# Chunked attention ahead of an expert layer: state summed from PSUM, the mask and a one-hot on ScalarE, a PSUM bank for VectorE's operands

## The chip, the cores and the metric

The kernel runs on one core of a Trainium2 chip. The metric is the device time of one launch in microseconds (us); lower is better. Five engines work side by side, each through its own list of instructions in order: TensorE (PE), VectorE (DVE), ScalarE (ACT), GpSimd (POOL), and SyncE (SP), whose list here is the queue of nearly all DMAs.

## The reference, cut to what matters

Three layers, one after the other. With B=4, H=8, S=768, D=40 the first is a recurrent attention; its output is 3072 tokens of 320 numbers.

```python
for t in range(S):
    m_new = np.maximum(f_gate[:, :, t] + m, i_gate[:, :, t])
    f_stab = np.exp(f_gate[:, :, t] + m - m_new)
    i_stab = np.exp(i_gate[:, :, t] - m_new)
    C = f_stab * C + i_stab * outer(vt, kt)
    n = f_stab * n + i_stab * kt
    y[:, :, t] = sigmoid(o_gate) * (C @ qt) / np.maximum(np.abs(n . qt), 1.0)
# expert layer: top 1 of 8 experts, d_ff 1024
logits = xn @ en.T / tau            # rows of x and expert_emb normalized
e = argmax(logits); gate_w = softmax(logits)[e]
out = gate_w * (relu(x @ w1[e]) @ w2[e])
# rational layer, d_ff 2048
h = x @ w_in
g = (a0 + a1 h + a2 h^2 + a3 h^3) / (1 + |b0||h| + |b1| h^2 + 1e-6)
return g @ w_out
```

## The kernel before, in words

**Attention.** The 3072 tokens are 24 tiles of 128 (tile t is chunk c = t % 6 of batch b = t // 6). Within a tile the recurrence is a product with a decay matrix: `s_scan` (L560) builds, for all eight heads, the 128 x 1024 matrix d of running products of the forget gates from fb, a broadcast of one tile's gates to all partitions (`load_f`, L351), and eight identities side by side. `s_score` (L337) makes the scores k·q in three matmuls, into three PSUM banks (phs[0], yb[0], yb[1]); `s_p` (L602) multiplies them into d, in three pieces; `s_out` multiplies by v (L621), adds the product of the carried state with the decayed q (qd, L629), and makes pc, this tile's addition to the state (L637). `s_state` carries the state on: pc has the products of all pairs of heads of a group of three, so the ones off the diagonal are masked out (L655, tm = pc * bmask), and cn = cn * fcol + tm in three pieces, one for each group of heads (L658). Where c is 0, one masked product makes cn (L652); where c is 5, there is no state to carry.

Each finished tile is then divided by its denominator (`s_abs` L674, `s_den1`, `s_den2`, `s_w` on POOL, `s_x` L693), transposed (`s_tr` L709), and routed: `s_logit` (L720), the winning expert oh (`s_arg`, L731 to L741), the position within the expert by two tiny matmuls, with a triangle and with ones (`s_rank` L753), and the running count (`s_count` L758). `s_pos` (L765 to L788) turns rank into two one-hot matrices, ohp (L781, 128 wide: the column in its group of 128) and ohj (L788), whose product (`s_map` L798) scatters token numbers into a map from position to token. `s_store` writes the tile to memory.

**What sets the order.** The loop `for step in range(-4, 24)` goes through a list written by hand, `plan`, of entries (lag, function): in each step every function runs for tile step - lag. The scan has lag -1, scores and s_p lag 0, s_out and s_state lag 1, the division lag 2, transposes 3, logits 4, the winner and s_rank 5, s_pos 6, s_map 7. What an engine gets in a step stands in its list in that order, and an instruction that waits holds up all behind it on its engine. Entries dv, pv, av take single instructions from side lists (the expert norms, the expert order, the first weights).

Ahead of the loop stands a prologue written out by hand (gates, their products, the first two tiles' scans and scores), behind it a drain, which finishes the last tiles and mixes in the first matmuls of the first expert (`pre_split` L257 transposes its gathered rows xj; `pre1`). The expert layer follows (w_load, `w_hi` L185, gemm1 L1471), with products of values split in high and low parts (`mm3`, L230), then the rational layer. `coef_load` and `dbl_load` start the transfers of the rational layer's coefficients and first weights; before, they are written behind the block that counts the tokens of each expert (L1527 to L1557).

## Time and profile before

| | us |
|---|---|
| runs of the kernel before | 820.78, 818.58, 820.72 (median 820.72) |
| the profiled execution, whole | 818.65 |
| its span, as the profile counts | 816.8 |
| busy in the span: PE, DVE, ACT, POOL | 762.5, 711.1, 489.7, 579.5 |

The span runs from the first to the last instruction that the profiler records; the time of the execution is 1.85 us longer. An engine's busy share is an average over three layers with different limits, so the rows further down are read stage by stage: prologue up to about 28 us, the loop to about 172, drain and first expert to about 222, the experts to about 350, the rational layer to the end. A row of a timeline gives the start and the length of a run of equal instructions (x3: three of them), the line, the operation, and output <- inputs with partitions x elements; in brackets stands the idle time of the engine before it and whom it waited for. The length counts to the end of the last one; since instructions overlap a little, the distance from one start to the next is what the engine spends.

### The profile page before, as it was taken

Reading aid. Unit: us, or ns where it says so; the run is one execution under the profiler, and the core shown is the slowest. Engines: PE = TensorE matmul, PEld = TensorE weight load, DVE = VectorE, ACT = ScalarE, POOL = GpSimd, SP = SyncE. Lnnn points to the kernel's source line nnn. Section 1 sums busy time; section 2 is a strip of 40 time slices with the busy share of each in tenths; the row PEclk is TensorE's granted clock in tenths of the full one; section 3 lists DMA queues with packets and bytes.
Section 4 is the critical chain, followed back from the end, with each engine's and each line's share of the span. In section 5 each row is a group of like instructions: output and inputs, shape, how many; then the busy total and the mean of one; then the engine's idle time right before and its main releaser. Section 6 shows DMA issues by size and latency. Waiting matters only on the chain.

```text
span 816.8 us, 14477 instructions
## 1 busy us (share of the span) xinstructions
PE 762.5 (93%) x4724; PEld 711.6 (87%) x4724; DVE 711.1 (87%) x1421; ACT 489.7 (60%) x839; POOL 579.5 (71%) x595
## 2 busy tenths in 40 slices
PE   8998888878789999999999899999999999999994
PEld 5787777768788788999999799999999999999983
DVE  7999999998669999998788898989888888889882
ACT  5344334433345655555657787787787877777872
POOL 6554443465447668679963688989899888989883
PEclk7899999988889999999999899999999999999998
DMA  8998787931747667688765030101000010000000
GB/s 199 263 233 248 222 240 214 263 114 49 209 121 212 198 180 225 201 272 270 251 206 187 1 118 21 42 1 49 1 26 25 17 33 9 17 9 17 1 25 24
DMA packets 86960, 102.37 MB, mean 125 GB/s; under 512 B 7915, under 2 KB 79219, under 8 KB 86880
## 3 DMA queue, kind: packets, MB, share of 16 engines
q1 hardware_dynamic: 82976, 88.63, 37.6%
q0 software_dynamic: 3904, 12.77, 4.8%
q8 instruction: 38, 0.62, 0.3%
q14 instruction: 42, 0.34, 0.1%
HBM read 84.01 MB, written 17.93 MB: 125 GB/s over the span
## 4 chain that ended last, share of the span: by engine, by line
PE 57%; DVE 21%; DMA 7%; issue 6%; POOL 4%; ACT 2%; SPq 2%; POOLq 0%; DVEq 0%; ACTq 0%
PE h L230 21%; PE yb L1308 6%; PE yb L1310 6%; PE ph L230 6%; PE yb L1309 6%; PE yb L1486 2%; PE yb L1487 2%; PE yb L1488 2%; DVE cn L658 2%; DVE ohp L781 1%; DMA raw<-in_w_in 1%; DMA r<-in_w 1%; POOL l L194 1%; DMA fb<-fz_d 1%; DVE xt L693 1%
## 5 line engine op out<-in xcount | busy, mean ns | idle before, releaser
L1248 POOL TENSOR_TENSOR U<-U,A 128x768 f32<-128x768 f32 (+1 forms) x65 | 119.0, 1830 | 30.8 <-ACT U L1240 26.1
L1310 PE MATMUL yb<-wo,gl 128*128 128x320 f32 x384 | 119.4, 311 | 1.8 <-POOL gl L1294 1.7
L1308 PE MATMUL yb<-wo,gh 128*128 128x320 f32 x384 | 119.2, 310 | 1.2 <-ACT gh L1291 1.2
L1294 POOL TENSOR_TENSOR gl<-P,gh 128x768 fp32r<-128x768 f32 x63 | 117.7, 1868 | 3.6 <-ACT gh L1291 3.0
L1309 PE MATMUL yb<-wo,gh 128*128 128x320 f32 x384 | 119.0, 310 | 0.0
L1224 ACT ACTIVATE P<-h,coef 128x768 f32<-128x768 f32 (+1 forms) x65 | 64.0, 984 | 73.4 <-PE h L230 73.4
L230 PE MATMUL h<-xh,winh 128*128 128x384 f32 x256 | 90.9, 355 | 3.9 <-DVE P L1257 3.8
L194 POOL TENSOR_TENSOR l<-r,h 128x384 fp32r<-128x384 f32 x64 | 63.7, 1017 | 38.5 <-ACT h L185 38.4
L1252 DVE TENSOR_TENSOR P<-P,h 128x768 f32<-128x768 f32 (+1 forms) x65 | 61.2, 942 | 29.6 <-ACT A L1232 24.9
L230 PE MATMUL h<-xh,winl 128*128 128x384 f32 x256 | 86.7, 339 | 0.0
L230 PE MATMUL h<-xl,winh 128*128 128x384 f32 x256 | 86.7, 339 | 0.0
L1310 PEld LDWEIGHTS yb<-wo,gl 128*128 128x128 f32 x384 | 72.5, 189 | 2.6 <-POOL gl L1294 2.6
L1308 PEld LDWEIGHTS yb<-wo,gh 128*128 128x128 f32 x384 | 72.6, 189 | 1.5 <-ACT gh L1291 1.5
L1309 PEld LDWEIGHTS yb<-wo,gh 128*128 128x128 f32 x384 | 72.5, 189 | 0.0
L1242 POOL TENSOR_SCALAR U<-A,coef 128x768 f32<-128x768 f32 x56 | 54.9, 981 | 21.9 <-ACT A L1232 21.2
L1486 PE MATMUL yb<-h,hh 128*128 128x320 f32 (+1 forms) x216 | 67.5, 313 | 3.0 <-DVE ysb L1500 3.0
L1487 PE MATMUL yb<-l,hh 128*128 128x320 f32 (+1 forms) x216 | 67.2, 311 | 0.0
L1257 DVE SCALAR_TENSOR_TENSOR P<-P,coef,h 128x768 f32<-128x768 f32 (+1 forms) x65 | 65.2, 1003 | 2.3
L1488 PE MATMUL yb<-h,hl 128*128 128x320 f32 (+1 forms) x216 | 67.0, 310 | 0.0
L1283 DVE SCALAR_TENSOR_TENSOR P<-P,coef,s 128x768 f32<-128x768 f32 (+1 forms) x62 | 62.0, 1000 | 1.7
L1275 DVE SCALAR_TENSOR_TENSOR U<-U,s 128x768 f32<-128x768 f32 (+1 forms) x62 | 58.0, 935 | 4.7 <-ACT s L1271 4.6
L230 PE MATMUL ph<-xh,h 128*128 128x256 f32 (+4 forms) x152 | 55.8, 367 | 6.4 <-DVE hl L1472 5.8
(590 smaller groups left out, 2322.4 us busy)
## 6 DMA issues: line engine op xcount, KB each, us to landing
fb<-fz_d SPq DMA_DIRECT2D x22, 512.0 KB
r<-in_w SPq DMA_DIRECT2D x32, 320.0 KB
r<-in_w SPq DMA_DIRECT2D x32, 256.0 KB
raw<-in_w_out SPq DMA_DIRECT2D x16, 320.0 KB
r<-in_w SPq DMA_DIRECT2D x64, 64.0 KB
raw<-in_w_in SPq DMA_DIRECT2D x32, 128.0 KB
x_rows<-xt SPq DMA_DIRECT2D x24, 164.5 KB
xt<-y_sorted SPq DMA_DIRECT2D x8, 481.5 KB
```

What stands on the lines that cost most here:

```text
L194: eng.tensor_tensor(out=l1[:, :, sl], in0=r1[:, :, sl], in1=h1[:, :, sl].bitcast(F32), op=ALU.subtract)
L230: mms = [nc.tensor.matmul(ps, lhsT=a, rhs=b, start=(i == 0), stop=(i == 7)) for i, (a, b) in enumerate(seq)]
L1224: r = nc.scalar.activation(out=part("P", m, i), in_=part("ph", m, i), func=AF.Identity, scale=coef[:, 3:4], bias=coef[:, 2:3])
L1248: eng.tensor_tensor(out=U, in0=U, in1=part("A", m, i), op=ALU.mult)
L1257: r = nc.vector.scalar_tensor_tensor(out=P, in0=P, scalar=coef[:, 1:2], in1=part("ph", m, i), op0=ALU.add, op1=ALU.mult)
L1294: eng.tensor_tensor(out=part("gl", m, i), in0=part("P", m, i), in1=part("gh", m, i).bitcast(F32), op=ALU.subtract)
L1308: nc.tensor.matmul(y, lhsT=gh[:, i, t], rhs=wh, start=first, stop=False)
L1309: nc.tensor.matmul(y, lhsT=gh[:, i, t], rhs=wl, start=False, stop=False)
L1310: nc.tensor.matmul(y, lhsT=gl[:, i, t], rhs=wh, start=False, stop=last)
L1486: nc.tensor.matmul(y, lhsT=hh[:, js], rhs=h2[:, half, :], start=(fb == 0), stop=False)
L1487: nc.tensor.matmul(y, lhsT=hh[:, js], rhs=l2[:, half, :], start=False, stop=False)
L1488: nc.tensor.matmul(y, lhsT=hl[:, js], rhs=h2[:, half, :], start=False, stop=(fb == NFB - 1))
```

## The change

It has six parts.

1. The state is summed straight from PSUM: cn = cn * fcol + pc, with no mask ahead of it and no tm. The mask moves behind it, to ACT: `s_mask` makes cm, the masked copy, in three products, and qd·c reads cm. `s_state` stands ahead of the scan.
2. The scores go into two banks instead of three, in four matmuls (384, 128, 256, 256 wide), and s_p multiplies two pieces of 512. The bank yb[1] that comes free is VectorE's: it holds three identities (vid), jt and the small tiles key, sj and dn. The scan is cut in three, over 3, 3 and 2 heads, with vid as its second operand.
3. ohp moves from VectorE to ACT, as two operations: dist = |iota + sj|, then Relu(tokf - tokf * dist).
4. `s_rank` moves from the end of lag 5 to lag 6, behind the scores; `s_map` behind the logits; in the drain the last `s_out` comes ahead of the last map, and `s_pre` behind both.
5. fz_d in memory is laid out by tiles, so that the load of fb is one row of 4 KB for each partition; the store of it is four DMAs for one, twice.
6. The prologue has the scans and scores of tiles 0 and 1 and s_out(0) ahead of the second half of the gates, with ten small idle products; `coef_load` and two `dbl_load` are written ahead of the counts.

```diff
@@ state, mask
             if c == 0:
-                nc.vector.tensor_tensor(out=cn, in0=pc, in1=mk, op=ALU.mult)
+                nc.vector.tensor_copy(cn, pc)
             else:
-                tm = lp.tile([120, H * V], F32, name="tm", bufs=1)
-                nc.vector.tensor_tensor(out=tm, in0=pc, in1=mk, op=ALU.mult)
                 for g, (h0, n) in enumerate(GR):
                     sl = slice(h0 * V, (h0 + n) * V)
                     nc.vector.scalar_tensor_tensor(
-                        out=cn[:, sl], in0=st["c", t][:, sl], scalar=fcol[:, b, g, c:c + 1], in1=tm[:, sl],
+                        out=cn[:, sl], in0=st["cn", t - 1][:, sl], scalar=fcol[:, b, g, c:c + 1], in1=pc[:, sl],
                         op0=ALU.mult, op1=ALU.add,
                     )
...
+        def s_mask(t):
...
+            for j in range(3):
+                hs = slice(j, H, 3)
+                nc.scalar.activation(
+                    out=ch[:, hs, :], in_=cv[:, hs, :], func=AF.Copy, scale=bmask[:, 0, j, 0:1]
+                )
+            st["c", t + 1] = cm
@@ the bank, scores, scan
+    vid, vjt, vkey, vsj, vdn = (
+        sr["yb"][1][:, a:a + n] for a, n in ((0, HALF), (384, JS), (392, NE), (400, 1), (408, H))
+    )
...
-        for g, (h0, n) in enumerate(GR):
...
+        pss = [v.rearrange("p (h t) -> p h t", t=CH) for v in (phs[0], sr["yb"][0])]
+        for g, h0, n in ((0, 0, 3), (1, 3, 1), (1, 4, 2), (2, 6, 2)):
...
-            nc.vector.tensor_tensor_scan(
-                out=d_.rearrange("p h t -> p (h t)"), data0=fb.rearrange("p h t -> p (h t)"),
-                data1=ident8.rearrange("p h t -> p (h t)"), initial=0.0, op0=ALU.mult, op1=ALU.add,
-            )
...
+            for h0, n in GR:
+                sl = slice(h0 * CH, (h0 + n) * CH)
+
+                nc.vector.tensor_tensor_scan(
+                    out=df[:, sl], data0=ff[:, sl], data1=(ident3 if t < 2 else vid)[:, 0:n * CH], initial=0.0,
+                    op0=ALU.mult, op1=ALU.add,
+                )
@@ fb and its store
-        fv = fz_d[b * H:(b + 1) * H, c * CH:(c + 1) * CH]
-        nc.sync.dma_start(out=fb, in_=fv.unsqueeze(0).broadcast_to([128, H, CH]))
+        nc.sync.dma_start(
+            out=fb.rearrange("p h t -> p (h t)"), in_=fz_d[t:t + 1, :].broadcast_to([128, H * CH])
+        )
...
-            nc.sync.dma_start(out=fz_d[:, a:z], in_=fzf[:, a:z])
+            for b in range(B):
+                nc.sync.dma_start(
+                    out=fz_d[b * NCH + ca:b * NCH + cz, :].rearrange("c (h t) -> h c t", t=CH),
+                    in_=fz[b * H:(b + 1) * H, ca:cz, :],
+                )
@@ one-hot
-                nc.vector.tensor_scalar(
-                    out=st["ohp", t], in0=niota, scalar1=st["sj", t][:, 1:2], scalar2=tokf[:, t:t + 1],
-                    op0=ALU.is_equal, op1=ALU.mult,
+
+                dist = ap.tile([128, 128], F32, name="dist", bufs=1)
+                nc.scalar.activation(out=dist, in_=iota, func=AF.Abs, bias=st["sj", t][:, 1:2])
+                nc.scalar.activation(
+                    out=st["ohp", t], in_=dist, func=AF.Relu, scale=ntokf[:, t:t + 1], bias=tokf[:, t:t + 1]
                 )
@@ plan
-            at(1, s_out), at(3, s_tr), at(4, s_logit), at(5, s_rank), at(5, s_keep),
-            at(-1, s_scan), dv, at(1, s_state), at(3, s_trc), at(2, s_x2),
+            at(1, s_out), at(3, s_tr), at(4, s_logit), at(7, s_map), at(7, s_first), at(5, s_keep),
+            at(1, s_state), at(-1, s_scan), dv, at(3, s_trc), at(2, s_x2), at(1, s_mask),
@@ drain
+        s_pos(z - 6, 3)
+        s_out(z)
+        s_map(z - 6)
+        s_abs(z)
+        s_pre(z)
         pre1(0)
-        s_map(z - 6)
-        s_out(z)
-        s_abs(z)
@@ rational layer
+        coef_load()
+        for i in range(2):
+            dbl_load(i)
 
         tc.mark_branch_hint_location("over", "LikelyTaken", mybir.ALL_ENGINES)
```

How it moves the instructions shows in three lists. First VectorE, one step in the middle of the loop, before (d is the decay matrix, ph the bank of pc, sj and ohp belong to the positions):

```order
L693 TENSOR_TENSOR xt<-pa,sg 128x320
L560 SCALAR_TENSOR_TENSOR d__1491<-fb,ident_97 128x1024
L655 TENSOR_TENSOR tm<-ph_119,bmask 120x328
L658 SCALAR_TENSOR_TENSOR cn<-cn,fcol,tm 120x123 x2
L658 SCALAR_TENSOR_TENSOR cn<-cn,fcol,tm 120x82
...
L776 SCALAR_TENSOR_TENSOR sj<-sj,rank 128x1
L602 TENSOR_TENSOR d__1491<-yb_113,d__1491 128x384
L781 TENSOR_SCALAR ohp<-niota,sj,tokf 128x128
```

The same place with the change:

```order
L730 TENSOR_TENSOR xt<-pa,sg 128x320
...
L678 SCALAR_TENSOR_TENSOR cn<-cn,fcol,ph_120 120x123 x2
L678 SCALAR_TENSOR_TENSOR cn<-cn,fcol,ph_120 120x82
L585 SCALAR_TENSOR_TENSOR d__1675<-fb,yb_115 128x384 x2
L585 SCALAR_TENSOR_TENSOR d__1675<-fb,yb_115 128x256
...
L814 SCALAR_TENSOR_TENSOR sj<-yb_115,rank 128x1
L627 TENSOR_TENSOR d__1675<-yb_114,d__1675 128x512
```

The state stands ahead of the scan, tm and ohp are gone, and scan, cn and sj have an operand in PSUM (yb_115 and ph_120 are banks).

Then TensorE, from the products for the state through the next scores, before:

```order
L637 MATMUL ph_119<-v_1418,n__1257 120x123 x2
L637 MATMUL ph_119<-v_1418,n__1257 120x82
L709 MATMUL px<-ident,xt 128x128 x3
L720 MATMUL plr<-enT,xT 128x8 x3
L753 LDWEIGHTS tri
L753 MATMUL plr<-oh,tri 128x8
L753 LDWEIGHTS ones
L753 MATMUL plr<-oacc,ones 128x8
L337 MATMUL ph_118<-bd,k__1178 128x384
L337 MATMUL yb_113<-bd,k__1178 128x384
L337 MATMUL yb_114<-bd,k__1178 128x256
```

And with the change:

```order
L746 MATMUL px<-ident,xt 128x128 x3
L757 MATMUL plr<-enT,xT 128x8 x3
L838 MATMUL plr<-ohj,ohp 128x32 x2
L343 MATMUL ph_119<-bd,k__1247 128x384
L343 MATMUL ph_119<-bd,k__1247 128x128
L343 MATMUL yb_114<-bd,k__1247 128x256 x2
L790 LDWEIGHTS tri
L790 MATMUL plr<-oh,tri 128x8
L790 LDWEIGHTS ones
L790 MATMUL plr<-oacc,ones 128x8
```

The rank's two matmuls have gone behind the scores, and the map's two ahead of them.

Last ACT, one step, with the change (before, it has none of cm, dist and ohp):

```order
L821 ACTIVATE dist<-iota,sj 128x128
L822 ACTIVATE ohp<-dist,tokf,ntokf 128x128
L707 ACTIVATE dn<-pa 128x8
L700 ACTIVATE sg<-n__1509 128x320
L783 ACTIVATE xt<-plr 128x8
L751 ACTIVATE xT<-px 128x384
L738 ACTIVATE sg,xt<-xt 128x320
L692 ACTIVATE cm<-cn,bmask 120x3x41 x2
L692 ACTIVATE cm<-cn,bmask 120x2x41
```

The mask's three products stand last in the step, behind the copy of the transposes and the squares of xt.

## Rows read from the trace of the kernel before

**Rows 1.** Windows: busy us (and instructions) of each engine, granted clock, DMA share, GB/s.
```profile
28.00:172.00 144.00, 127.74 (x888) 108.81 (x887) 141.89 (x407) 52.65 (x146) 65.83 (x113) 0.98 0.79 224
172.00:222.00 50.00, 41.39 (x269) 38.05 (x270) 41.89 (x154) 17.32 (x49) 28.10 (x32) 0.83 0.46 136
350.00:816.00 466.00, 449.24 (x2802) 439.58 (x2801) 395.61 (x541) 336.90 (x482) 383.04 (x293) 0.99 0.22 69
```

**Rows 2.** VectorE's timeline: the scans of tile 3 and of tile 23.
```profile
31.79 2.27 DVE L560 TENSOR_TENSOR_SCAN d__448<-fb,ident 128x1024 f32<-128x1024 f32 x1
...
176.50 2.52 DVE L560 TENSOR_TENSOR_SCAN d__2119<-fb,ident 128x1024 f32<-128x1024 f32 x1
```

**Rows 3.** VectorE's groups by line, 28 to 172 us: busy us, mean ns | idle.
```profile
L658 DVE SCALAR_TENSOR_TENSOR cn<-cn,fcol,tm 120x123 f32<-120x123 f32 (+1 forms) x42 | 19.9, 527 | 0.5
L781 DVE TENSOR_SCALAR ohp<-niota,sj,tokf 128x128 fp32r<-128x128 f32 x16 | 11.0, 688 | 0.0
L655 DVE TENSOR_TENSOR tm<-ph,bmask 120x328 f32<-120x328 f32 x14 | 6.6, 471 | 0.0
L776 DVE SCALAR_TENSOR_TENSOR sj<-sj,rank 128x1 f32<-128x1 f32 x16 | 5.4, 338 | 0.0
```

**Rows 4.** VectorE's timeline: a state sum with nothing of POOL's beside it.
```profile
133.52 0.47 DVE L655 TENSOR_TENSOR tm<-ph,bmask 120x328 f32<-120x328 f32 x1
134.03 0.82 DVE L658 SCALAR_TENSOR_TENSOR cn<-cn,fcol,tm 120x123 f32<-120x123 f32 x3
134.76 0.16 DVE L758 TENSOR_TENSOR oacc<-oacc,oh 128x8 bf16<-128x8 bf16 x1
```

**Rows 5.** VectorE's timeline in the prologue: a scan whose first operand is in PSUM.
```profile
17.45 2.29 DVE L560 TENSOR_TENSOR_SCAN d__318<-fb,ident 128x1024 f32<-128x1024 f32 x1 [2.53 <-PE fb L450]
```

**Rows 6.** TensorE's timeline: two steps without a wait.
```profile
44.81 0.89 PE L337 MATMUL ph<-bd,k__305 120*128 120x384 f32 x2
...
50.68 0.89 PE L337 MATMUL ph<-bd,k__470 120*128 120x384 f32 x2
...
92.20 0.80 PE L629 MATMUL pa<-cn,qd 120*128 120x123 f32 x6
92.83 0.80 PE L637 MATMUL ph<-v,n__833 128*120 128x123 f32 x6
...
96.05 0.48 PE L798 MATMUL plr<-ohj,ohp 128*128 128x32 f32 x2
96.38 2.03 PE L621 MATMUL pa<-v,d__1075 128*128 128x82 f32 x16
98.24 0.80 PE L629 MATMUL pa<-cn,qd 120*128 120x123 f32 x6
```

**Rows 7.** TensorE's waits, 28 to 184 us: us in total, times, longest.
```profile
PE plr L753 <- DVE oh L741: 12.8, 15, 1.5
PE pa L629 <- DVE cn L658: 3.4, 14, 0.5
```

**Rows 8.** ACT's groups by line and shape, 100 to 170 us.
```profile
L714 ACT ACTIVATE xT<-px 128x384 f32<-128x384 f32 x10 | 4.8, 484 | 0.0
```

**Rows 9.** Timelines of the drain and the first expert: VectorE, TensorE, ACT.
```profile
179.45 3.04 DVE L658 SCALAR_TENSOR_TENSOR cn<-cn,fcol,tm 120x123 f32<-120x123 f32 x3
...
179.53 0.90 PE L257 MATMUL plr<-ident,xj 128*128 128x128 f32 x3 [1.49 <-DMA xj<-x_rows,xid]
227.91 0.58 PE L230 MATMUL ph<-xh,h 128*128 128x256 f32 x1 [4.21 <-DVE hl L1472]
...
174.59 0.84 ACT L185 ACTIVATE h<-r 128x768 fp32r<-128x768 f32 x1 [6.30 <-DMA r<-in_w]
```

**Rows 10.** Windows for the DMA engines' share and GB/s, the last two columns.
```profile
28.00:164.00 136.00, 121.09 (x843) 103.33 (x843) 133.96 (x384) 51.02 (x140) 62.30 (x107) 0.97 0.84 237
103.00:106.00 3.00, 3.00 (x30) 3.00 (x29) 2.63 (x14) 0.94 (x1) 2.01 (x4) 1.00 1.05 213
108.00:110.00 2.00, 2.00 (x12) 1.48 (x10) 2.00 (x3) 1.92 (x6) 0.00 (x0) 1.00 1.07 366
```

More of the change, by code (lines that the diff above doesn't have):

```diff
@@ L81 @@
     ekey = const.tile([128, NTILE], F32, name="ekey")
-    niota = const.tile([128, 128], F32, name="niota")
+    iota = const.tile([128, 128], F32, name="iota")
+    ntokf = const.tile([128, NTILE], F32, name="ntokf")
     jt = const.tile([128, JS], F32, name="jt")
@@ L105 @@
     over = dram.tile([NT, 1], I32, name="over")
-    fz_d = dram.tile([NH, S], F32, name="fz_d")
+    fz_d = dram.tile([B * NCH, H * CH], F32, name="fz_d")
     cp_d = dram.tile([NH, S], F32, name="cp_d")
@@ L112 @@
     acon = actx.enter_context(tc.tile_pool(name="acon", bufs=1))
-    ident8 = acon.tile([128, H, 128], F32, name="ident8")
+    ident3 = acon.tile([128, HALF], F32, name="ident3")
     bmask = acon.tile([120, 3, 3, V], F32, name="bmask")
@@ L379, with products @@
         nc.vector.memset(idle, 0.0)
-        for _ in range(12):
-            nc.tensor.matmul(phs[0], lhsT=idle[:, 0:128], rhs=idle, start=True, stop=True)
+        def products(n, out):
+            for _ in range(n):
+                nc.tensor.matmul(out, lhsT=idle[:, 0:128], rhs=idle[:, 0:out.shape[1]], start=True, stop=True)
+        products(12, phs[0])
         mt = gp.tile([NH, S + 1], F32, name="mt")
@@ L732, in s_arg @@
             elif i == 1:
[L733 removed]
+                st["key", t] = own(t, 5, vkey, lambda: ap.tile([128, NE], F32, name="key", bufs=3))
                 nc.vector.scalar_tensor_tensor(
@@ L888 @@
             blocks(0, i, 0, CH)
+        spread(1)
+        s_scan(0)
+        s_v(0)
+        s_score(0)
+        s_scan(1)
+        s_v(1)
+        gpctx.close()
+        ps_a = actx.enter_context(tc.tile_pool(name="ps_a", bufs=2, space=PSUM))
+        ps_1 = actx.enter_context(tc.tile_pool(name="ps_1", bufs=1, space=PSUM))
+        plf = ps_1.tile([128, 512], F32, name="plr")
+        plr = plf[:, 0:9 * NE].rearrange("p (a e) -> p a e", e=NE)
+        for c in (1, 2):
+            for i in range(5):
+                blocks(0, i, c * CH, (c + 1) * CH)
+        for i in range(2):
+            s_p(0, i)
+        products(10, phs[1][:, 424:])
+        s_score(1)
+        s_out(0)
         half = gate_exps(3, NCH)
@@ L891 @@
         next(en)
-        s_scan(0)
-        s_v(0)
-        s_score(0)
-        spread(1)
-        for c in (1, 2):
-            for i in range(5):
-                blocks(0, i, c * CH, (c + 1) * CH)
+        load_qk(1, nc.sync)
+        load_kvo(2)
         for _ in half:
             pass
-        load_qk(1, nc.sync)
-        load_kvo(2)
         load_f(3)
-        for g in range(3):
-            s_p(0, g)
-        s_scan(1)
-        s_v(1)
-        s_score(1)
-        for g in range(3):
-            s_p(1, g)
+        for i in range(2):
+            s_p(1, i)
         gate_columns(3, NCH)
@@ L1543, in counts @@
                 nc.vector.tensor_tensor(out=pend, in0=pend, in1=past, op=ALU.subtract)
+        coef_load()
+        for i in range(2):
+            dbl_load(i)
         tc.mark_branch_hint_location("over", "LikelyTaken", mybir.ALL_ENGINES)
@@ L1556 @@
                 x_prep(0, kk, (*phs, pt0)[kk][:, NP:])
-        coef_load()
-        for i in range(2):
-            dbl_load(i)
         dbls = dbl()
```

72 lines of the change are left out of this document (41 added, 31 removed).

## The prediction

> **What bounds the kernel now.** I read the windows by stage first, then VectorE's timeline over the loop, then the waits and the timeline of TensorE, then the DMA shares. After the attention TensorE is busy for 449.24 of 466 us [rows 1]; what comes after the loop and its drain is TensorE's, and the change leaves it alone. A gain made earlier passes through it unchanged. In the attention loop, from 28 to 172 us, it is VectorE that is full: 141.89 of 144 us, beside 127.74 on TensorE, 65.83 on POOL and 52.65 on ACT [rows 1]. The scan of tile 3 starts at 31.79 and that of tile 23 at 176.50 [rows 2]: 20 steps in 144.71 us, **7.24 us a step**, of which VectorE works 141.89 / 20 = 7.09. Everything in the loop that shortens VectorE's step shortens the loop, until the next resource is full. So two sums are needed: VectorE's step after, and the floors of the others.
>
> **VectorE's step.** The groups by line give totals over the window [rows 3].
> - The masked product tm goes: 14 times, 6.6 us. Where c is 0 a copy takes the place of a product of one width; I put nothing there.
> - The one-hot ohp goes to ACT: 16 times, 11.0 us.
> - The state sum cn stays, but one input now comes from PSUM. Its 42 pieces take 19.9 us, 1.42 us for a tile's three. The same three pieces take 0.82 us at 134.03 (0.73 until the next operation starts) and 3.04 us at 179.45 [rows 4, 9], so what they cost depends on what runs beside them, and not on their width. The trace has no cn with a PSUM input. Below: the three cost no less than tm's 0.47 us, one operation of their summed width, also with one input in PSUM [rows 3, 4], 14 x (1.42 - 0.47) = 13.3 us saved. Above: nothing is saved. I take the undisturbed 0.73 us, as the product with a PSUM input keeps the same 471 ns over all 14 [rows 3]: 14 x (1.42 - 0.73) = 9.7 us. The Trainium skill ("SBUF — State Buffer", Who interferes with whom) says that a VectorE instruction with two SBUF inputs contends with a GpSimd one that reads SBUF, and that one with a single SBUF input does not. By that rule my value holds in every step; without it the term could be zero, which is the rival C below.
> - The small difference sj takes 5.4 us for 16 columns of one element [rows 3], 0.34 us each, for nothing that its size explains. With one operand in PSUM it saves between 0 and 5.4 us; I take half, 2.7.
> - The scan becomes three instructions. Three pieces against one of the same width is cn's 0.73 against tm's 0.51 from start to start [rows 4], so 0.11 us for each further start: two, 20 times, 4.4 us lost. The score products go from three to two: 2.2 us won. That the scan reads a second operand in PSUM I cost at nothing: a scan whose first operand lay in PSUM took 2.29 us [rows 5], the others 2.27 and 2.52 [rows 2].
> Sum: 6.6 + 11.0 + 9.7 + 2.7 - 4.4 + 2.2 = 27.8 us, and (141.89 - 27.8) / 20 = **5.7 us** a step on VectorE.
>
> **TensorE's floor.** TensorE twice runs through a whole step without a wait: from 92.20 to 98.24 us with the map products, 6.04, and from 44.81 to 50.68 without them, 5.87 [rows 6]; the map is 96.38 - 96.05 = 0.33, so 6.04 to 6.20; I take 6.1. Two tiles in six lack the qd·c or the pc products, 0.63 us (92.20 to 92.83): 0.2 off the mean. The fourth score matmul adds between nothing and one more instruction; 0.1. The floor is **6.0 us**, above VectorE's. Its waits today are those of the rank matmul for oh, 12.8 us, and of qd·c for cn, 3.4 us [rows 7], 0.8 us a step. The change moves the rank a step later, behind the scores, where oh has been ready since the previous step, and replaces the wait for cn by one for ACT's cm. In return two engines that are about equally long now wait on each other, where one was in front.
>
> **ACT, POOL and DMA.** ACT gets three masking products of 123 or 82 columns and two of 128 a tile, between a third of the 484 ns of a 384-wide one and all of it [rows 8]: 0.8 to 2.4 us a step on an engine that works 52.65 / 20 = 2.6. It stays below TensorE, and what hides the products is the rest of its step, over 3 us of idle time; it is gone only if ACT waits for loads there. POOL keeps its work. The DMA engines are the next cover: from 28 to 164 us their share is 0.84 [rows 10], 114.2 us (up to 172 us it is 0.79 of 144 [rows 1], no more in total, so the loads of the loop end by 164), for 136 / 7.24 = 18.8 steps, **6.1 us a step**, over the floor of TensorE. The load of fb is a third of that: 512 KB of 512-byte pieces, which become rows of 4 KB. While an fb load and the short coefficient rows behind it are under way the share is 1.05 at 213 GB/s; with the wide rows of q, k, v it is 1.07 at 366 [rows 10]. At these two rates fb takes 2.46 and 1.43 us, so the step on the DMA engines comes to between 6.1 and 5.05. I take the lower, as the rows differ most in width.
>
> **The step.** TensorE's floor of 6.0 plus half of the 0.8 us that it waits in a step today: **6.4 us**. Saved: (7.24 - 6.4) x 20 = **16.8 us**.
>
> **Before and after the loop.** In the prologue scans and scores come ahead of the second half of the gates. VectorE idles 2.53 us there ahead of a scan [rows 5], which work written earlier can fill in part; against it the fz_d store, split in four, puts six DMAs more into SP's queue, ahead of the loads of the first steps. I put +1 us, from -2 to +3. In the drain (172 to 222 us, TensorE busy 41.39 of 50 [rows 1]) the last cn without contention saves 3.04 - 0.73 = 2.3 us, and TensorE's wait of 1.49 us for xj [rows 9] gets a place behind the last outputs; against that ACT, which waited 6.30 us for a weight load r [rows 9], now has the mask of tile 21 and ohp near that wait. I put +2 us, from -2 to +5. The transfers of the rational layer that are written ahead of the counts change no place in SP's queue against the weight loads, and the coefficients land where they did: the 4.21 us that TensorE waits at 227.91 [rows 9] stay. Nothing.
>
> **Sum.** 16.8 + 1 + 2 = 19.8 us from the 818.65 us of the profiled execution (span 816.8): 798.85. The median of the runs lies 2.07 us above that execution; I go half way and say **800 us**.
>
> **Rivals.**
> - A, the DMA engines pace. If wide rows are no faster, 6.1 us a step at a share of 0.92, half way between today's 0.84 and full, give 6.6 us: saved 12.8 + 3, **804 us**. For it: the share is 0.84 already. Against it: 213 beside 366 GB/s. The Trainium skill ("DMA: Bandwidth & Descriptors", Specifications) states that transfers reach line rate from 512 bytes on, which fb's pieces have; by that rule relaying fz_d brings nothing, and the rows of the trace speak against it.
> - B, no waits are left: 6.0 us a step, saved 24.8 + 3, **792 us**. For it: VectorE was paced to within 0.15 us of its work. Against it: there was then no second engine as long.
> - C, the state sum stays disturbed and sj keeps its price: VectorE 5.7 + 0.49 + 0.13 = 6.3, and with the same 0.4 us of waits 6.7: saved 10.8 + 3, **806 us**. Against it: tm's constant 471 ns.
> - D, slower: the mask on ACT closes a loop. pc is followed by cn (0.73), by cm on ACT (0.8 to 1.4), by qd·c (0.63) and pc again (0.63) on TensorE's ordered queue: 2.8 to 3.4 us. Should ACT hold the mask back by over 7.24 - 3.4 = 3.8 us in every step, behind the blocks of a q that it waits for, the loop is longer than today's step; at 4.3 us it is 7.7: lost 9.2, won 3, **826 us**. For it: the mask is last on ACT's list in a step. Against it: ACT works under 40% of the window, and the blocks come once in three tiles.
> - The change does nothing that can be told: gains on VectorE meet a DMA share near 1, about 819 us.
>
> **Chances.** Forecast 0.50, A 0.15, B 0.15, C 0.12, D 0.04, nothing 0.04. A measurement of this kernel tells about 0.3% (2.5 us) from no change: faster by more 0.92, within it 0.04, slower by more 0.04. The range reaches from B with the upper ends before and after the loop (24.8 + 3 + 5 saved, **786**) to A and C with their lower ends: C with -2 in the prologue and none in the drain saves 8.8, 809.9 us or 811 by the median; **812**.
>
> **What would show it.** The distance of the scans in the loop: 6.4 us if I am right, 6.6 or more with a DMA share near 1 for A, or with cn's three pieces above 1.2 us for C. The three cn pieces at about 0.75 us in every tile. The rank matmul without a wait, a new wait of qd·c for cm on ACT, and TensorE busy for over 93% of the loop. Fb's stretch of the DMA windows over 300 GB/s. The wait for hl at the start of the expert products as long as before. I am wrong if the step is above 7 us, if the mask on ACT is what TensorE waits for in most steps, or if time is lost behind 222 us.

## Result and the profile after

| | before | after |
|---|---|---|
| median of four runs, side by side | 819.65 us | 811.1 us |
| ratio, 95% interval | | 0.9912, 0.9883 to 0.994 |
| the same on a second chip (13 and 10 runs) | 816.9 us | 812.2 us, 0.9954, 0.9928 to 0.998 |
| profiled execution and its span | 818.65, 816.8 us | 811.32, 809.5 us |

The ratios are the estimates on record, with their intervals; they are not the quotients of the two medians, which are 0.9896 and 0.9942.

Faster, as forecast, and at the upper end of the range of 786 to 812 us: by 8.5 us on one chip and 4.7 on another, where 20 were forecast. The windows after, with the columns of [rows 1] (us, then busy time and instructions of PE, PEld, DVE, ACT, POOL, the granted clock, DMA share, GB/s):

```profile
28.00:172.00 144.00, 134.00 (x954) 119.89 (x953) 125.98 (x427) 83.35 (x247) 68.77 (x122) 0.93 0.81 240
172.00:222.00 50.00, 38.66 (x238) 36.27 (x236) 29.26 (x119) 23.43 (x65) 22.22 (x27) 0.77 0.45 133
350.00:809.00 459.00, 442.27 (x2764) 432.90 (x2762) 389.96 (x527) 332.98 (x474) 377.09 (x287) 0.99 0.21 66
```

VectorE is no longer full (125.98 of 144 us), TensorE has gone from 127.74 to 134.00, ACT from 52.65 to 83.35; and TensorE's clock, 0.98 in this window before, is 0.93. VectorE's timeline gives the scans of tiles 3, 20 and 23 (start, length):

```profile
33.06 2.36 DVE L585 TENSOR_TENSOR_SCAN d__482<-fb,yb 128x384 f32<-128x384 f32 x3
...
142.36 2.37 DVE L585 TENSOR_TENSOR_SCAN d__1931<-fb,yb 128x384 f32<-128x384 f32 x3
...
167.60 2.37 DVE L585 TENSOR_TENSOR_SCAN d__2243<-fb,yb 128x384 f32<-128x384 f32 x3
```

In the kernel before, tile 20's scan starts at 152.04, the count of the tokens that ends the drain at 212.59, and TensorE resumes after its wait for hl at 227.91; after, these are at 207.03 (the count) and 222.12 (hl). So the 7.3 us between the two spans come from:

| stretch | before | after | won | forecast |
|---|---|---|---|---|
| start to scan of tile 3 | 31.79 | 33.06 | -1.3 | +1 |
| tile 3 to tile 20, 17 steps | 120.25 | 109.30 | +10.95 | } +16.8 |
| tile 20 to tile 23, 3 steps | 24.46 | 25.24 | -0.8 | } |
| scan of tile 23 to the count | 36.09 | 39.43 | -3.3 | +2 |
| the count to the end of hl's wait | 15.32 | 15.09 | +0.2 | 0 |
| the rest | 588.89 | 587.38 | +1.5 | 0 |

The drain is here the stretch from the scan of tile 23 to the count. A step in the long stretch takes 109.30 / 17 = 6.43 us: the 6.4 of the forecast. But the steps are not alike. From scan to scan, tile 3 onwards, us:

```
before  6.6 6.5 5.9 7.0 6.8 6.9 7.7 8.3 6.8 7.1 6.8 6.9 7.7 8.3 6.8 7.1 6.8 6.9 8.3 9.3
after   7.1 6.2 5.9 5.3 5.9 7.9 6.2 6.4 7.3 5.4 5.9 8.5 6.2 6.3 7.3 5.4 5.9 7.6 9.9 7.8
```

After, from tile 6 to tile 20, two steps in three take 5.3 to 6.4 us, and every third 7.3 to 8.5. In these ACT makes blocks of the next half batch's q. One such step, on ACT's, VectorE's and TensorE's timelines (in brackets idle time and whom it waited for):

```profile
84.39 0.94 ACT L692 ACTIVATE cm<-cn,bmask 120x123 f32<-120x123 f32 x3
85.22 1.75 ACT L332 ACTIVATE bd<-q__976,bmask 120x768 f32<-120x768 f32 x2
86.88 0.39 ACT L821 ACTIVATE dist<-iota,sj 128x128 f32<-128x128 f32 x1
87.30 0.49 ACT L822 ACTIVATE ohp<-dist,tokf,ntokf 128x128 fp32r<-128x128 f32 x1
87.70 0.15 ACT L707 ACTIVATE dn<-pa 128x8 f32<-128x8 f32 x1
...
87.89 0.17 DVE L717 TENSOR_SCALAR yb<-dn 128x8 f32<-128x8 f32 x1 [1.30 <-ACT dn L707]
88.10 0.23 DVE L771 SCALAR_TENSOR_TENSOR yb<-plr,mx,kio 128x8 f32<-128x8 f32 x1
...
89.46 1.10 PE L343 MATMUL ph<-bd,k__975 120*128 120x384 f32 x4 [0.24 <-ACT xt L783]
```

The mask (0.94), the blocks (1.75), dist and ohp (0.39, 0.49) stand on ACT ahead of dn, a copy of eight columns that takes 0.15 us. VectorE, whose list is in order, waits 1.30 us for it, and with it the key (L771), and behind the key wait TensorE's next logits, since the key is made from the bank they write. Over the loop, in the waits of the kernel after (us in total, times, longest):

```profile
DVE yb L717 <- ACT dn L707: 9.1, 8, 2.4
...
PE plr L757 <- DVE yb L771: 3.5, 4, 1.0
PE plr L790 <- ACT xt L783: 2.2, 2, 1.6
PE ph L343 <- ACT bd L332: 1.4, 1, 1.4
```

TensorE's waits for oh and cn [rows 7] are gone, and a wait for cm, which the forecast expected in their place, is not among its waits. In three stretches of the loop TensorE's clock is low; in the kernel before there are two short ones. Windows around them, of the kernel after and then of the kernel before:

```profile
28.00:40.00 12.00, 10.13 (x51) 9.07 (x50) 10.59 (x32) 4.56 (x14) 6.79 (x12) 0.72 0.88 267
70.00:73.00 3.00, 3.00 (x11) 2.15 (x10) 3.00 (x10) 2.13 (x9) 0.72 (x1) 0.50 0.93 327
148.00:160.00 12.00, 10.38 (x50) 9.23 (x50) 9.22 (x36) 3.03 (x11) 4.18 (x8) 0.57 0.46 156
```
```profile
28.00:40.00 12.00, 11.49 (x78) 9.45 (x78) 11.78 (x28) 2.62 (x9) 6.06 (x11) 1.00 0.79 252
86.00:90.00 4.00, 3.11 (x7) 1.88 (x7) 4.00 (x7) 2.80 (x8) 1.22 (x3) 0.61 0.80 252
144.00:148.00 4.00, 3.51 (x10) 2.27 (x10) 4.00 (x14) 1.62 (x6) 0.55 (x2) 0.62 1.01 294
```

A share of 0.57 of full speed is mostly the lower level, 1.2 of 2.4 GHz. Ahead of the first stretch TensorE waited 1.42 us for the blocks bd, ahead of the last 0.82 us for the key and 1.70 for ACT's xt.

### The profile page after: what moved, and what is told of

Same layout as the page of the kernel before. It is cut to its first block, busy times and chain, and to the rows that moved or that the text cites. A ratio compares the mean times of both kernels' runs of the same rounds, so it can differ in the third digit from the quotient of the medians.

```text
span 809.5 us, 14673 instructions
## 1 busy us (share of the span) xinstructions
PE 762.2 (94%) x4782; PEld 719.8 (89%) x4782; DVE 682.5 (84%) x1407; ACT 522.6 (65%) x947; POOL 573.6 (71%) x596
## 4 chain that ended last, share of the span: by engine, by line
PE 60%; DVE 16%; ACT 5%; issue 5%; DMA 5%; POOL 3%; SPq 2%; POOLq 0%; DVEq 0%; ACTq 0%
PE h L236 21%; PE ph L236 7%; PE yb L1359 6%; PE yb L1357 6%; PE yb L1358 6%; PE yb L1535 2%; PE yb L1536 2%; PE yb L1537 2%; PE pa L643 2%; DMA r<-in_w 1%; ACT bd L332 1%; DVE hl L1521 1%; DMA q__1248<-in_qT 1%; PE h L1160 1%; DVE ct L1441 1%
## 5 line engine op out<-in xcount | busy, mean ns | idle before, releaser
L1301 DVE TENSOR_TENSOR P<-P,h 128x768 f32<-128x768 f32 (+1 forms) x65 | 61.2, 942 | 29.1 <-ACT A L1281 24.5
```

## Experiments

Theory 1 after the comparison of the traces was that ACT is the new wait: q comes late, and what TensorE and VectorE need stands behind it on ACT. Theory 1a was that the order on ACT alone is enough, as dn stands last. Rivals: 2, VectorE and TensorE are about equally long and wait on each other by themselves, which was the forecast's reason for 6.4 us; 3, the DMA engines are full. The ratios are to the kernel before, taken side by side on the same chip; the changed kernel itself was taken on two chips, 0.9912 and 0.9954, so a difference of less than about 0.004 between chips is not told here. e1 to e4 shared a chip, and so did e0 with e5 to e7, e8 to e10, and e11 with e13 and e14. "Step" is the mean from tile 3 to tile 20, "20 to 23" the three steps behind them, "drain" the stretch from the scan of tile 23 to the count, all from one profiled execution of each kernel; the step differs by 0.1 us between executions of the same loop (e7 and e11).

| run | edit to the changed kernel | ratio (95%) | step us | 20 to 23 | drain |
|---|---|---|---|---|---|
| e0 | none | 0.9954 (0.9928-0.998) | 6.41 | 24.5 | 39.9 |
| e1 | q a step earlier | 0.9923 (0.9891-0.9955) | 6.39 | 22.4 | 39.5 |
| e2 | state back on VectorE | 0.993 (0.9902-0.9957) | 6.61 | 23.5 | 37.2 |
| e3 | fb in 512-byte pieces | 0.9958 (0.9933-0.9982) | 6.52 | 23.1 | 39.7 |
| e4 | ohp back on VectorE | 1.0043 (1.0014-1.0072) | 6.83 | 25.3 | 43.4 |
| e5 | dn first on ACT | 0.9841 (0.9803-0.9879) | 6.11 | 22.9 | 39.5 |
| e6 | e5, q a step earlier | 0.9835 (0.9798-0.9871) | 6.21 | 21.4 | 40.5 |
| e7 | e6, weights' split last, first blocks ahead of the mask | 0.9838 (0.9803-0.9873) | 6.00 | 21.5 | 38.3 |
| e8 | drain in the old order | 0.998 (0.9942-1.0019) | 6.49 | 22.6 | 43.6 |
| e9 | rank back ahead of the scores | 0.9996 (0.9958-1.0034) | 6.81 | 25.8 | 38.9 |
| e10 | coefficients' operations later | 0.9907 (0.9878-0.9936) | 6.51 | 26.1 | 38.2 |
| e13 | e5, state back on VectorE | 0.9896 (0.9853-0.9938) | 6.43 | 23.1 | 38.6 |
| e14 | e5, ohp back on VectorE | 1.0011 (0.9988-1.0034) | 6.67 | 23.2 | 43.3 |
| e11 | e7 and e10 | 0.9792 (0.9744-0.984) | 6.11 | 21.4 | 39.9 |

**e1, q a step earlier.**
```diff
-            at(-3, s_f), at(-2, s_kvo), at(-3, s_qk), at(-2, s_c), at(6, s_store), ...
+            at(-3, s_f), at(-4, s_q), at(-2, s_kvo), at(-3, s_qk), at(-2, s_c), at(6, s_store), ...
...
         def s_qk(t):
             if t > 3 and t % 3 == 0:
-                load_qk(t // 3, nc.sync)
+                load_k(t // 3)
+        def s_q(t):
+            if t > 3 and t % 3 == 0:
+                load_q(t // 3, nc.sync)
```


> The changed kernel, with the load of q issued one step (one tile) earlier than that of k. Theory 1 (late q): with the change ACT waits 1.4 to 3.2 us for q in six of the eight half batches, and behind the blocks of q stand the mask and the copies that TensorE waits for; the steps with blocks take 7.3 to 8.5 us, the others 5.3 to 6.4. If so, the waits for q are below 0.5 us each, the 17 steps from the scan of tile 3 to that of tile 20 fall from 6.43 to about 6.0 us, and the time from 811 to 800 to 805 us. Theory 2 (VectorE and TensorE wait on each other, q only happens to be late): the waits for q go, the step stays at 6.3 to 6.4 us, 809 to 811 us. Theory 3 (the DMA engines are full, share 0.95 from 60 to 90 us): q comes earlier, fb or k later by as much; 809 to 813 us.

Measured: ACT's waits for q are no longer among its longer waits, the steps at 7.9 and 8.5 us become 7.3, and nothing below 7.3 changes; in all 6.39 us a step. The first step, at a low clock from 40 to 44 us, rises to 8.4. q was late, but behind it the order on ACT holds as long: theory 1 alone falls. VectorE's waits for dn stay, 8.5 us in all. The run also answers a rival that no theory named, that the low clock makes the steps long: from 60 to 120 us the clock is 1.00, and the steps of 7.3 us are still there.

```profile
60.00:120.00 60.00, 57.55 (x438) 51.58 (x438) 55.40 (x196) 38.01 (x112) 30.60 (x55) 1.00 0.94 268
```

**e2, the state back on VectorE.** Masked product and sum as in the kernel before, `s_mask` out of the plan.
```diff
-            at(1, s_state), at(-1, s_scan), dv, at(3, s_trc), at(2, s_x2), at(1, s_mask),
+            at(1, s_state), at(-1, s_scan), dv, at(3, s_trc), at(2, s_x2),
...
```


> The changed kernel, with the state made as in the kernel before: masked product and sum on VectorE, no mask on ACT, the rest as changed. Theory 1 and 2: the state from PSUM is worth its share of VectorE's step, 6.6 + 9.7 us less what TensorE's floor takes back; the time is 816 to 822 us. Theory of the mask (the mask on ACT, held behind blocks of q, is itself what delays TensorE): less than 3 us lost, 808 to 814 us, and TensorE's half-clock stretches at 32 to 40 and 150 to 160 us are gone.

Measured: 0.2 us a step lost, the time no different from the changed kernel's within what the two chips tell. The time, 811.7 us, is the one that the theory of the mask gave, but the low clock near 36 us, which it said would go, stays (28 to 60 us: 0.89). Nor does the run give back all of the 16.3 us (tm 6.6, cn 9.7) that the forecast's sum has for the state: the sum cn stays ahead of the scan, and its 45 pieces take 14.1 us, 0.31 each, where the kernel before takes 0.47 and the changed kernel 0.27. With tm's 7.4 us VectorE has 9.5 us more to do than in the changed kernel.

```profile
L678 DVE TENSOR_TENSOR tm<-ph,bmask 120x328 f32<-120x328 f32 x15 | 7.4, 491 | 0.1
L681 DVE SCALAR_TENSOR_TENSOR cn<-cn,fcol,tm 120x123 f32<-120x123 f32 (+1 forms) x45 | 14.1, 368 | 0.5
```

**e3, fb in pieces of 512 bytes.**
```diff
-        nc.sync.dma_start(
-            out=fb.rearrange("p h t -> p (h t)"), in_=fz_d[t:t + 1, :].broadcast_to([128, H * CH])
-        )
+        fv = fz_d[b * H:(b + 1) * H, c * CH:(c + 1) * CH]
+        nc.sync.dma_start(out=fb, in_=fv.unsqueeze(0).broadcast_to([128, H, CH]))
...
```


> The changed kernel, with fz_d as in the kernel before, so that fb is loaded as eight pieces of 512 bytes for each partition and stored by one DMA for a half. If the wide rows carry the step (fb at over 300 GB/s against 213): the DMA share from 60 to 90 us goes to 1, q comes later by about 1 us, the step grows by 0.3 to 0.6 us, 816 to 823 us. If wide rows are no faster, as the rule of 512 bytes has it: 810 to 812 us, and the prologue a little shorter.

Measured: a ratio of 0.9958 beside 0.9954 and 0.9912, a step of 6.52. The page's line on the DMA queue of SP (packets, MB, share of the 16 engines over the span), of this run and of the changed kernel:

```profile
q1 hardware_dynamic: 82976, 88.63, 37.5%
```
```profile
q1 hardware_dynamic: 63424, 88.63, 37.1%
```

The wide rows are 19,552 packets fewer, and 0.375 x 808.9 - 0.371 x 809.5 = 3.0 us less work for the engines, 0.14 us for each of the 22 loads, a seventh of the 1.03 us that the forecast took. Even that did not count, as DMA was not what the step waited for: theory 3 falls, at a share of 0.88 in the stretch from 60 to 120 us of the changed kernel, where e5 ran faster at 0.96.

**e4, ohp back on VectorE.**
```diff
-                dist = ap.tile([128, 128], F32, name="dist", bufs=1)
-                nc.scalar.activation(out=dist, in_=iota, func=AF.Abs, bias=st["sj", t][:, 1:2])
-                nc.scalar.activation(
-                    out=st["ohp", t], in_=dist, func=AF.Relu, scale=ntokf[:, t:t + 1], bias=tokf[:, t:t + 1]
-                )
+                nc.vector.tensor_scalar(
+                    out=st["ohp", t], in0=iota, scalar1=st["sj", t][:, 1:2], scalar2=tokf[:, t:t + 1],
+                    op0=ALU.is_equal, op1=ALU.mult,
+                )
...
```


> The changed kernel, with the one-hot ohp made by VectorE in one operation, as before, in the place it had. If VectorE is still what the steps wait for: 0.5 to 0.7 us a step over 16 steps, 816 to 822 us. If ACT is (theory 1: ACT's list is what TensorE waits behind in the steps with blocks): 0.8 us less on ACT a step, 808 to 812 us.

Measured: 0.4 us a step and 4 us in the drain lost, at a ratio of 1.0043 (1.0014 to 1.0072) to the kernel before. Without the move of ohp the change gains nothing; ACT's 0.9 us for it is not what hurts.

**e0 and e5, dn first on ACT.** The second pair of blocks moves behind the gate of the next step (for the first half batch it stays).
```diff
-            at(7, s_pos, 3), at(2, s_abs), at(1, s_sig), at(0, s_blocks, 0), av,
+            at(2, s_abs), at(7, s_pos, 3), at(1, s_sig), at(1, s_blocks, 1), at(0, s_blocks, 0), av,
...
```


> The changed kernel itself, beside its variants on one chip. All theories: a ratio of 0.991 to the kernel before, as measured; the steps from the scan of tile 3 to that of tile 20 at 6.4 us, with 7.3 to 8.5 us in the steps with two blocks of q, and half-clock stretches near 36 and 155 us if these belong to the kernel and not to one execution.

> The changed kernel with another order on ACT: the denominator's copy dn first in the step, ahead of the two operations of ohp, and the second pair of blocks of q behind the gate of the next step instead of at the end of its own. Theory 1a (VectorE waits for dn, which stands on ACT behind mask, blocks and ohp, 11.1 us in nine waits, and TensorE's logits wait for VectorE): VectorE's wait for dn goes to under 2 us in all, the steps that took 7.3 us take about 6.3, those at 7.9 and 8.5 us (q late as well) about 7; the time is 1 to 0.5% under the changed kernel's, some 804 to 807 us on its chip. Theory 2 (VectorE and TensorE wait on each other by themselves): the long steps stay at 7.3 and more, no difference.

Measured: e0 has the same step of 6.41 us and the low clock near 36 us, but its later low stretch lies elsewhere (90 to 120 us at 0.89): where it falls belongs to the execution. e5 takes the long steps between tile 4 and tile 20 to 6.0 to 6.7 us, and 1.1% off the changed kernel. Its first step, from tile 3 to 4, is 8.2 us. The wait for dn in e5, us in total:

```profile
DVE yb L719 <- ACT dn L709: 1.3, 2, 0.7
```

1.3 us where the changed kernel has 9.1, for the same work on every engine. Theory 2 falls: two engines of about 6 us do not wait on each other by themselves. The edit moves two things on ACT, dn and the second pair of blocks, and how much each brings was not tried alone.

**e6 and e7.** e6 is e5 with e1; e7 adds the following.
```diff
-            ..., at(1, s_blocks, 1), at(0, s_blocks, 0), av,
+            ..., at(1, s_blocks, 1), at(0, s_blocks, 0),
...
-            ..., at(3, s_trc), at(2, s_x2), at(1, s_mask),
-            at(-1, s_v), at(-1, s_decay), at(0, s_blocks, 2), pv, pv,
+            ..., at(3, s_trc), at(2, s_x2), at(0, s_blocks, 2), at(1, s_mask), av,
+            at(-1, s_v), at(-1, s_decay), pv, pv,
```


> e5 and the load of q a step earlier. Theory 1 and 1a together: neither wait is left, all steps from tile 3 to 20 are at TensorE's own 5.4 to 6.3 us, 6.0 us in the mean against 6.43, which is 7 us, ratio to the kernel before 0.980 to 0.985. Theory 3 (DMA engines full): the step stays at 6.3 us and the DMA share is above 0.95 all through the loop.

> e6, and the split of the first expert's weights (which waits 4.1 us on ACT for its load at 163 us, with mask and transposes behind it) last in ACT's step instead of early in it; in the first steps the blocks of q ahead of the mask, which waits 2.25 us for the state there. If the half-clock stretches come from these two holds of ACT, the stretch at 32 to 40 us and the steps of tiles 21 to 23 (25.2 us for three) go to full clock and 20 to 21 us: 4 to 7 us less than e6. If they come from TensorE's own gaps in the drain and the prologue, no more than 1 us less.

Measured: the steps of e7 are 6.00 us in the mean, 5.3 to 6.7, at a clock of 1.00 from 28 to 40 us, and three to tile 23 take 21.5. In the time e5, e6 and e7 can't be told apart: the 4 to 7 us that e7 should have gained, if the low clock came from the two holds on ACT, did not come. e6 already takes 21.4 us for the three steps to tile 23, with the weights' split in its old place. The higher mean of e6, 6.21, is its first step of 9.4 us, with a low clock from 40 to 46 us; from tile 4 to tile 20 the mean is 5.98, 6.01, 5.96 and 5.95 in e5, e6, e7 and e11. The loop of e7 in the windows:

```profile
28.00:154.00 126.00, 121.77 (x918) 109.74 (x919) 121.14 (x411) 77.73 (x232) 63.63 (x114) 0.99 0.91 263
```

TensorE and VectorE are both busy for over 96% of it, and in e6 TensorE is busy for all 60 us from 60 to 120. This is the floor of 6.0 us for TensorE that the forecast worked out (rival B).

**e8, the old order of the drain.**
```diff
         s_pos(z - 6, 3)
-        s_out(z)
-        s_map(z - 6)
-        s_abs(z)
-        s_pre(z)
         pre1(0)
+        s_map(z - 6)
+        s_out(z)
+        s_abs(z)
```
(and `s_pre` back into the plan)


> The changed kernel with the drain ordered as in the kernel before: the first expert's rows transposed in the last step of the loop, its first matmuls and the last map ahead of the last outputs. In the changed kernel the drain from the scan of tile 23 to the count of the tokens takes 39.4 us where it took 36.1. If the new order of the drain is the cause: 36 to 37 us, and the time 2 to 3 us less than the changed kernel's (ratio 0.991 where that has 0.995 on this chip). If it is the lower clock (0.77 where it was 0.83), which follows from TensorE waiting for VectorE and ACT there whatever the order: 38 to 40 us and no difference.

Measured: 43.6 us, longer than 39.4 and outside both expectations, as TensorE now waits 2.8 us for xj and 2.1 for ohp. The new order isn't what makes the drain longer.

**e9, the rank back at lag 5.**
```diff
-            ..., at(0, s_score), at(6, s_rank), at(0, s_rest),
+            ..., at(0, s_score), at(0, s_rest),
...
-            ..., at(4, s_logit), at(7, s_map), at(7, s_first), at(5, s_keep),
+            ..., at(4, s_logit), at(7, s_map), at(7, s_first), at(5, s_rank), at(5, s_keep),
...
```


> The changed kernel with the two matmuls of the rank back at the end of lag 5, ahead of the next scores. If the rank's wait for oh is what TensorE loses to VectorE (12.8 us in the kernel before): TensorE waits 0.5 to 0.8 us a step for oh again, the step from tile 3 to 20 goes from 6.4 to 6.8 us, 5 to 8 us more. If that wait only filled a gap that stays (TensorE then waits for dn's chain instead): under 2 us more.

Measured: 0.4 us a step, all of the gain again. In the waits of this run TensorE has it back:

```profile
PE plr L790 <- DVE macc L843: 7.7, 8, 1.5
PE plr L790 <- DVE oh L778: 3.0, 4, 1.0
```

10.7 us in all, of the 12.8 of [rows 7]; 7.7 of them are now put down to macc, the map's sum on VectorE.

**e10, the coefficients later.**
```diff
-        s3_coef()
         for n in range(NB + LAG2):
...
+            if n == 6:
+                s3_coef()
```


> The changed kernel with the two operations that turn the coefficients of the rational layer moved from the head of the expert loop to its seventh step. TensorE idles 4.2 us for hl at the head in both kernels, as ACT waits 3.4 us for the coefficients and POOL as long. If that idle time is the coefficients': hl's wait goes to under 1 us and the time falls by 3 to 4 us. If the transfers behind which the coefficients stand are waited for anyway (weights, tokens): TensorE waits as long for something else, under 1 us gained.

Measured: from the count to the end of hl's wait 12.63 us instead of 15.1. TensorE's waits at the head of the experts, of the changed kernel and of this one:

```profile
PE ph L236 <- DVE hl L1521: 5.9, 2, 4.2
```
```profile
PE ph L236 <- DVE hl L1521: 3.2, 2, 1.7
```

So 2.5 us of the idle time are the coefficients', which the changed kernel writes earlier without any effect: SP starts them 8.3 us after the count (9.0 before), behind the same weight loads. They are had by asking for the values later. At the head TensorE still waits 1.5 us for hl where under 1 was expected, and the time, 0.9907, is not told from the changed kernel's on its first chip.

**e13 and e14, one move undone where ACT holds nothing back.** e5 with the edits of e2 and e4.


> e5 (dn first on ACT) with the state made as in the kernel before, on VectorE. In the changed kernel giving the state back cost 0.2 us a step. If that was so little because ACT held VectorE anyway (theory 1a), then without the hold VectorE is full again: its step by the rows of the changed kernel is 5.7 + 0.33 (tm) + 0.5 (cn disturbed), about 6.5 us from tile 3 to 20 against 6.1 in e5, 7 us in the time (ratio about 0.992). If the state never mattered: 6.1 to 6.2 us a step, ratio 0.984 to 0.987.

> e5 with the one-hot ohp back on VectorE. In the changed kernel this cost 0.4 us a step and 4 us in the drain. If VectorE's work is what it costs: 0.5 to 0.7 us a step against 6.1 in e5, and again 4 us in the drain, 11 us in all (ratio 0.996 to 1.0). If it cost by VectorE's ordered list (the map waits for it, TensorE's scores wait behind the map): the step stays under 6.3 us and only the drain is longer, ratio 0.988 to 0.99.

Measured: 6.43 and 6.67 us a step against 6.11 in e5. Both moves count by VectorE's work once the hold is gone, 0.32 and 0.56 us, close to the 6.5 us a step and the 0.5 to 0.7 that were expected; in the changed kernel e2 and e4 cost 0.2 and 0.4. The time of e13 is 0.9896 for 0.992, that of e14 1.0011 for 0.996 to 1.0. The windows from 60 to 120 us, in the order changed kernel, e5, e13, e14:

```profile
60.00:120.00 60.00, 57.34 (x429) 51.27 (x428) 53.61 (x191) 37.54 (x111) 28.43 (x52) 0.97 0.88 258
```
```profile
60.00:120.00 60.00, 58.37 (x453) 52.89 (x451) 58.31 (x201) 40.55 (x122) 32.39 (x59) 1.00 0.96 286
```
```profile
60.00:120.00 60.00, 57.43 (x439) 51.30 (x438) 58.75 (x194) 32.49 (x93) 28.45 (x51) 1.00 0.87 265
```
```profile
60.00:120.00 60.00, 54.32 (x402) 47.44 (x403) 59.45 (x184) 30.79 (x93) 26.66 (x49) 1.00 0.83 251
```

VectorE is held at 53.61 us in the changed kernel and works 58.31 in e5; with either move undone it is at 58.75 and 59.45 of 60, and TensorE falls behind, to 57.43 and 54.32.

**e11, all together.** e7 with e10's edit.


> e7 and the coefficients' operations moved back as in e10: all the waits that the experiments named are taken away together. If they add up: e7's 0.984 less 2.5 to 4 us, ratio 0.978 to 0.981, about 799 us where the kernel before takes 817; TensorE's wait for hl under 2 us. If what one saves the next wait takes: 0.983 to 0.985.

Measured: 798.2 us beside 818.3, ratio 0.9792 (0.9744 to 0.984), faster than both kernels. It is at the middle of what was expected if the waits add up, but the interval reaches into e7's, so that e10's edit adds to e7 is not shown by the time alone. TensorE's wait for hl at the head is 1.5 us, where e7 has 5.0.

## Why the prediction was wrong in size

**What bounds the kernel.** Right: VectorE was the bound, and with the order on ACT put right TensorE is the next. e13 and e14 show VectorE at 98 to 99% again when either move is undone.

**VectorE's terms.** Right, nearly all: from tile 3 to tile 20 VectorE works 98.44 / 17 = 5.8 us a step, where 5.7 was forecast. The groups by line of VectorE, 28 to 172 us, that answer to [rows 3]:

```profile
L678 DVE SCALAR_TENSOR_TENSOR cn<-cn,fcol,ph 120x123 f32<-120x123 f32 (+1 forms) x45 | 12.0, 323 | 2.3 <-PE ph L659 2.3
L814 DVE SCALAR_TENSOR_TENSOR sj<-yb,rank 128x1 f32<-128x1 f32 x17 | 2.5, 149 | 0.0
```

Three pieces of cn take 0.80 us, 0.72 from start to start, where 0.73 was taken; sj fell from 0.34 to 0.15 us, half, as taken. By the rule of the Trainium skill ("SBUF — State Buffer", Who interferes with whom) cn with one input in PSUM should not be disturbed by GpSimd, and the trace agrees: 0.27 us a piece in the mean of all 45 where it was 0.47. With both inputs in SBUF, in the kernel before and in e2, the three pieces take 0.82 us wherever no arithmetic of POOL runs beside them, and 1.02 to 1.77 us beside POOL's products; with one input in PSUM they take 0.80 us also beside them:

```profile
97.13 1.08 DVE L658 SCALAR_TENSOR_TENSOR cn<-cn,fcol,tm 120x123 f32<-120x123 f32 x3
96.85 0.74 POOL L583 TENSOR_TENSOR v<-v,d__1158 128x328 f32<-128x328 f32 x1 [3.45 <-DVE d__1158 L560]
```
```profile
83.38 0.80 DVE L678 SCALAR_TENSOR_TENSOR cn<-cn,fcol,ph 120x123 f32<-120x123 f32 x3
83.50 0.72 POOL L620 TENSOR_TENSOR qd<-q__719,c__795 120x256 f32<-120x256 f32 x1
```

But e2 shows that the new place alone brings most of this: with cn ahead of the scan POOL's products fall beside it in only four of fifteen tiles, and a piece takes 0.31 us though both inputs are in SBUF. The forecast gave the term to PSUM alone. The scan in three pieces takes 2.37 us and not 2.28, which is under half of the 0.22 us counted.

**TensorE's floor.** Right: 6.0 us, reached from tile 4 to tile 20 by e5, e6, e7 and e11 (5.95 to 6.01).

**The step.** This is where it failed: the "half of the 0.8 us that it waits in a step today", added to the floor as two engines of equal length waiting on each other. The number came out (6.43 for 6.4) by luck, as two errors cancelled: the 0.4 us of mutual waiting is not there (5.95 to 6.01 us in e5, e6, e7 and e11), and a wait of the same size that had been put at nothing is. That wait is VectorE's for dn, on ACT, in one step of three, 9.1 us in all: dn is last behind what the change put there. I had priced the load on ACT (0.8 to 2.4 us a step; the five operations take 0.94 + 0.39 + 0.49 = 1.8) and put it at nothing, hidden in over 3 us of idle time unless ACT waited for loads. It did wait, 1.4 to 3.2 us for q in each of six half batches, but e1 without these waits has the same steps of 7.3 us, and e5, with another order and the same work, is 1.1% faster. ACT is at 58% of the window and was still what others waited for, by its order. The list of ACT that stands ahead of the prediction shows dn behind dist and ohp; what stands in front of it and who waits for it was not followed.

**The end of the loop.** In the sum the missing time lies behind these steps. Of the 12.5 us between the 19.8 forecast and the 7.3 measured, 0.5 are the 17 steps, 6.0 the three steps behind them, 5.3 the drain and 2.3 the prologue; 1.7 came back behind. The 6.4 us were applied to 20 steps, and the last three took 25.2 us, not 19.2. The first of them has blocks of q (7.6 us, with 1.51 us of VectorE's wait for dn). In the other two TensorE has no idle time:

```profile
149.98:159.85 9.87, 9.87 (x48) 8.72 (x47) 7.09 (x29) 2.44 (x9) 3.45 (x6) 0.57 0.35 130
159.85:167.60 7.75, 7.75 (x59) 6.94 (x59) 6.96 (x29) 3.45 (x12) 2.84 (x5) 1.00 0.30 78
```

The first runs at a low clock, 0.57; in e1, at 1.00, the same step takes 8.2 us. And VectorE has 29 operations in each, where the 17 steps have 19 in the mean, because the experts' order is made there: 7.1 and 7.0 us of work against 5.8. A mean step does not hold for these two, and in no run do the three take less than 21.4 us. ACT's wait for the first weights [rows 9] is still there, 4.1 us in the last step, but the steps do not hang on it: e6, whose ACT waits 5.3 us for them, takes 21.4 us, and e7, where the weights' split is last in ACT's step, 21.5.

```profile
ACT h L191 <- DMA r<-in_w: 5.3, 1, 5.3
```

In the changed kernel it reaches TensorE behind the scan of tile 23, in the drain:

```profile
169.62 0.17 PE L790 MATMUL plr<-oh,tri 128*128 128x8 bf16 x1 [1.65 <-ACT xt L783]
```

**Prologue and drain.** -1.3 where +1 was put, -3.3 where +2. In the prologue the mask waits 2.25 us on ACT for the first state with blocks of q behind it, which TensorE's scores wait for; the clock then fell. That this is the loss is not shown: e10, with the same prologue and the same wait of 1.43 us for the blocks, has scan 3 at 31.4 us, earlier than the kernel before, and a clock of 1.00 from 28 to 40 us. e7, with these blocks ahead of the mask, has scan 3 at 31.2 us and the next 6.7 later, at full clock; e11, with the same loop, has 31.1 and 8.6, at 0.72. So this part changes with the execution by as much as was to be explained. In the drain TensorE is busy for 32.28 us, where it was 30.01, and idle 7.15 against 6.08, at a clock of 0.74 and 0.76. Its work is nearly the same, 198 matmuls for 196, but the first expert's products were caught more by the low clock, as the first group shows, before and after:

```profile
L230 PE MATMUL ph<-xh,h 128*128 128x256 f32 x18 | 6.4, 355 | 0.0
```
```profile
L236 PE MATMUL ph<-xh,h 128*128 128x256 f32 x18 | 7.4, 413 | 0.6 <-ACT xh L264 0.6
```

That its new order is not the cause is shown (e8). ACT's weights are behind 1.65 us of the idle time; what else makes it, and why the clock was low where it was, was not tried. In e7, where ACT does not wait for the weights, the drain still takes 38.3 us, so the cause of most of its loss stays open.

**Rivals.** A, DMA paces: no, at 0.88 to 1.00 of share (60 to 120 us, e6 the highest) it stayed behind TensorE. The rule of the Trainium skill ("DMA: Bandwidth & Descriptors", Specifications), line rate from 512 bytes on, fits the runs better than my reading of 213 beside 366 GB/s: e3 costs nothing that can be told. The low rate was not fb's pieces: with wide rows a stretch in which fb and the short coefficient rows are under way is at 221 GB/s, not over 300 as forecast, and the same stretch of e3, with the 512-byte pieces, at 217.

```profile
80.00:83.00 3.00, 3.00 (x31) 3.00 (x29) 2.87 (x16) 1.12 (x2) 2.80 (x6) 1.00 1.09 221
```

B, the floor without waits: it was there to be had, from e5 to e7. C: no. D, slower by the mask: the mask closed no loop, but its mechanism, ACT holding back what is needed, with blocks of q in front, is the one that held VectorE; I had only asked it of cm, not of dn.

**Coefficients.** Right that their place in the program brings nothing; the wait stayed, 4.18 us where it was 4.21.

## What to carry to other kernels

When work is moved to an idle engine, its sum is not the price: write down for that engine what stands behind the moved work in its list and who waits for each, above all for small results like an eight-column copy, and put those first. Here that order alone was worth as much as the whole change (e5 against e0). And a mean step should be taken apart, by its cycle (here three tiles) and by what single steps do besides (here the last two), before one waiting time or one saving is spread over all steps.
